# Query sketches in 64x64 tiles instead of 64x32, with the remainder's two batches as the outer loop

## The chip, the cores and the metric

The kernel runs on one core of a Trainium2 chip. The metric is device time in microseconds (us); lower is better. The engines are TensorE (PE, matrix products; its weight loads are listed as PEld), VectorE (DVE), ScalarE (ACT), GpSimd (POOL) and SyncE (SP, which issues most DMAs). All data are float32.

## The reference

Polysketch attention over 4 batches, 4 heads, 1088 tokens and 32 channels, then a GELU layer of 128 to 2048 to 128 channels over all 4352 tokens.

```
phi(x):  a = S1 x,  b = S2 x                # 8 numbers each
         features = outer(a, b)             # 64 numbers
kv  = phi(k)^T v          z = sum over tokens of phi(k)
x   = phi(q) kv / (phi(q) z + 1e-6)         # heads side by side: 128 channels
out = gelu(x w_in) w_out                    # 2048 hidden channels
```

What the change touches is the *query sketch*: for every query token and head, the products a and b with the two sketch matrices, and with them a product for the denominator.

## The kernel before, in words

**Chunks.** The queries go in chunks of 512 tokens of one batch: chunks 0 to 7 (two for each of the 4 batches). The last 64 tokens of all four batches together make chunk 8, the *remainder* (its halves have 128 columns where those of a main chunk have 256). Chunks 0 and 1 go another way at the start of the kernel; the sketch in question is made for chunks 2 to 8.

**The long middle.** From about 20 us on, the kernel is a list of steps, one for each chunk and each of 16 blocks of 128 hidden channels (`steps`, L962). In each step PE makes a hidden product (`hidden`, L715, product at L721), ScalarE takes it through GELU (L728), and PE multiplies earlier results by w_out (`two_products`, L792, product at L805, which uses a scheme with fewer products over sums that GpSimd makes at L770 to L773). What else has to be done for the chunks that follow (turning queries, sketches, key features, attention) is put into *slots* between the steps by hand (L964 to L1129). At the end of the kernel every engine is told to keep the order of the text (L1216 to L1222). So the order of PE's work is that of the program.

**The sketch** (`query_sketch`, L566, product at L578). `qT[n]` (from `query_turn`, L520) holds the chunk's queries with the channels of the heads in the partitions: rows 0 to 63 and 64 to 127 belong to two head pairs (`c`), the columns to two halves (`s`). `S_abc[b]` (L472; filled in `spread_sketches`, L475, and per batch in `sketch_of_z`, L489) is the stationary operand, 128 partitions x 2 (`fh`) x 2 (`r`) x 16: for each half `fh` of the first factor a and each head `r` of the pair, 4 numbers for a, 4 for the denominator and 8 for b. So 32 columns for each `fh`. Before the change a matmul takes 64 rows and 32 columns of weights, and 256 columns of queries. Its place in the array is the row half `c` and one of four column groups, `q4 = 2*s + fh`; that is a tile of 64x32, of which eight fit. A main chunk has 2 x 2 x 2 = 8 matmuls. In the remainder `m` is 2: each half `s` holds two batches `i` of 64 columns, whose weights differ, which makes 16 matmuls, with `s` as the outermost loop. The head pair `c` chooses the bank of PSUM, the column group its partitions.

**What reads it.** `query_outer` (L584) turns the sketch on VectorE (L590) and makes the query features. `attend` (L617; products at L633, in 64x32 tiles) multiplies them by kv; `take_x` (L638) copies the result with ScalarE (L644) to xT, which the hidden products of that chunk read.

**Where it stands.** At step t - 1 ahead of a chunk's own steps PE does, in this order:
- chunk 2 (L1082, L1083): the sums of kv (`kv_sum`, L440, product at L437 in 128x32 tiles), then the sketch.
- chunks 3 and 5 (`sketch_and_attend`, L1010): the sketch of n, the attention of n - 1, then the key features of the next batch (`features_of_all`, L970, product at L976 in 64x32 tiles).
- chunk 4 (`kv_and_attend`, L1048, then L1118): kv sums, attention of chunk 3, then the sketch.
- chunks 6 to 8 together (`last_sketches`, L1016): kv sums, attention of chunk 5, then the sketches of 8, 6 and 7.

The early part of the kernel has products in other tile shapes: `key_products` (L382) and `numerators_by_token` (L656) in 64x64 tiles, `expand_products` (L543) in 32x64. The products of hidden layers at L721 and L805 are in 128x64 tiles for most of the kernel.

Of the kernel before, what the change touches and what calls it, by code (L numbers as in the profile page):

```python
# [16 lines left out]
def kernel(  # L17
# [18 lines left out]
    pe, dve, act, pool, sp = nc.tensor, nc.vector, nc.scalar, nc.gpsimd, nc.sync  # L36
# [6 lines left out]
    NP = H // 2  # L43
# [23 lines left out]
    def work_banks():  # L67

        return wps.tile([128, 2, CW], FP, name="w_ps")
# [96 lines left out]
    def words(a):  # L166

        return (a, 1) if a.dtype == FP else (a.bitcast(U32), 2)
# [18 lines left out]
    for i, s in enumerate((S1, S2)):  # L187
        s, e = words(s)
# [283 lines left out]
    S_abc = [big.tile([128, 2, 2, 2 * R], FP, name=f"S_abc{b}") for b in range(B)]  # L472
# [44 lines left out]
    qT, qp, xT = {}, {}, {}  # L517
# [43 lines left out]
    def batch_of(n, s, i):  # L561
        return n // NCH if n < NMAIN else i * 2 + s
# [3 lines left out]
    def query_sketch(n, ps=None, tok=None):  # L566

        ps = work_banks() if ps is None else ps
        W = width[n]
        tok = ps[:, :, CW // 2:] if tok is None else tok  # L570
        m = 1 if n < NMAIN else B // 2
        N = W // 2 // m
        for s in range(2):
            for i in range(m):
                for fh in range(2):
                    for c in range(NP):
                        rows, q4 = slice(c * 64, (c + 1) * 64), 2 * s + fh
                        pe.matmul(ps[q4 * 32:(q4 + 1) * 32, c, i * N:(i + 1) * N],  # L578
                                  lhsT=S_abc[batch_of(n, s, i)][rows, fh].rearrange("p r x -> p (r x)"),
                                  rhs=qT[n].rearrange("p h j t -> p (h j t)")[rows, (s * m + i) * N:(s * m + i + 1) * N],  # L580
                                  start=True, stop=True)
        sketched[n] = ps, tok

    def query_outer(n):  # L584
# [308 lines left out]
    r = Rounding(SR)  # L893
# [116 lines left out]
    def sketch_and_attend(n):  # L1010

        ps = work_banks()
        query_sketch(n, ps)
        attend(n - 1, ps[:, :, CW // 2:])

    def last_sketches(b):  # L1016

        z_sum(b)
        fold_z(b)
        banks = work_banks()  # L1020
        kv = banks[:, 1, CW // 2 + 128:]
        kv_sum(b, kv)
        attend_products(NMAIN - 3, banks)
        query_sketch(NMAIN, banks[:, :, CW // 2:], banks)
        take_x(NMAIN - 3)
        take_kv(b, kv)
        two = work_banks()
        query_sketch(NMAIN - 2, two, banks)
        query_sketch(NMAIN - 1, two[:, :, CW // 2:], two)
        query_outer(NMAIN)  # L1030
# [59 lines left out]
    for n in range(3, NCHUNK):  # L1090

        t = (n - 1) * NF
# [69 lines left out]
    for t in range(len(steps) + LAG):  # L1162
# [35 lines left out]
        if t < len(steps):  # L1198
            n, fi = steps[t]
            hidden(n, fi, by_halves=t >= 18 and (n < NMAIN or fi < 5))  # L1200
        if t < len(steps) and steps[t][0] < NMAIN and steps[t][1] % NB == NB - 1:
            n, b = steps[t][0], steps[t][1] // NB
# [50 lines left out]
```

## Time and profile before

| | us |
|---|---|
| median of 3 runs | 259.8 (259.49 to 260.06) |
| the profiled execution's own time | 258.95 |
| its span, first to last instruction | 257.1 |
| PE busy | 253.1 (98%) |
| POOL, DVE, ACT busy | 164.1, 151.0, 115.2 |
| mean granted TensorE clock | 1.000 |

Busy times are unions: an engine with two instructions in flight is counted once. On PE many matmuls run side by side in different tiles of the array, and the record of each lasts from its start to the modelled arrival of its last result, so lengths of records overlap and don't add up to time. What adds up is the distance from the start of one group to the start of the next. The page's chain of work follows the end of the kernel back from what released each step. The timeline merges neighbouring instructions of one line and shape: start, length until the last end, and their number.

### The profile page before, as it was taken

How to read it: one execution, taken by the hardware profiler on the slowest of the kernel's cores; microseconds unless marked ns; L12 is line 12 of the kernel's file. 1: busy time of each engine (PE TensorE's matmuls, PEld its weight loads, DVE VectorE, ACT ScalarE, POOL GpSimd, SP SyncE). 2: the span in 40 equal slices, each digit the busy share in tenths (PEclk: the TensorE clock that was granted, in tenths of full speed). 3: DMA queues.
4: the chain of work that ended last, by engine and by line, in shares of the span. 5: the costliest groups of instructions: out<-in, count | busy, mean ns of one | idle time of the engine just before them, and what ended most of it. 6: DMA issues, size and time to landing. Idle time of an engine off the chain costs nothing.

```text
span 257.1 us, 5763 instructions
## 1 busy us (share of the span) xinstructions
PE 253.1 (98%) x2331; PEld 135.2 (53%) x2331; DVE 151.0 (59%) x313; ACT 115.2 (45%) x224; POOL 164.1 (64%) x173
## 2 busy tenths in 40 slices
PE   8999999999999999999999999999999999999995
PEld 7856444255454545454444455445544444445794
DVE  3896888969698996580278976399307000700330
ACT  4675766533535333533335332623444334433442
POOL 3504007799968777587758774787758777877300
PEclk9999999999999999999999999999999999999999
DMA  7479738720000101101000002000200200020020
GB/s 209 138 213 378 163 93 223 208 75 13 3 0 15 28 1 26 18 13 30 3 0 3 0 13 35 0 1 3 41 3 8 32 3 1 7 36 0 3 41 20
DMA packets 29594, 13.48 MB, mean 52 GB/s; under 512 B 21888, under 2 KB 27776, under 8 KB 29568
## 3 DMA queue, kind: packets, MB, share of 16 engines
q1 hardware_dynamic: 29392, 13.05, 20.4%
q8 instruction: 18, 0.29, 0.5%
q10 hardware_dynamic: 176, 0.07, 0.1%
q14 instruction: 8, 0.07, 0.1%
HBM read 10.88 MB, written 2.23 MB: 51 GB/s over the span
## 4 chain that ended last, share of the span: by engine, by line
PE 98%; ACT 0%; issue 0%
PE h_ps L721 45%; PE o_ps L805 33%; PE o_ps L856 5%; PE w_ps L853 3%; PE w_ps L437 1%; PE w_ps L578 1%; PE w_ps L888 1%; PE w_ps L633 1%; PE w_ps L543 1%; PE o_ps L426 1%; PE h_ps L735 1%; PE w_ps L976 1%; PE w_ps L656 0%; PE h_ps L333 0%; PE w_ps L333 0%; PE w_ps L467 0%
## 5 line engine op out<-in xcount | busy, mean ns | idle before, releaser
L721 PE MATMUL h_ps<-xT,w_in 128*64 128x512 f32 (+3 forms) x514 | 136.9, 576 | 0.0
L728 ACT ACTIVATE block<-h_ps 128x512 f32<-128x512 f32 (+1 forms) x128 | 73.0, 571 | 117.3 <-PE h_ps L721 115.3
L721 PEld LDWEIGHTS h_ps<-xT,w_in 128*64 128x64 f32 (+1 forms) x514 | 41.9, 142 | 30.6 <-issue 11.8
L805 PE MATMUL o_ps<-block,w_out 128*64 128x256 f32 x224 | 57.5, 379 | 0.0
L770 POOL TENSOR_TENSOR bits_low<-block 128x512 f32<-128x512 f32 x28 | 35.9, 1283 | 27.8 <-ACT block L728 27.8
L805 PEld LDWEIGHTS o_ps<-block,w_out 128*64 128x64 f32 x224 | 30.5, 137 | 38.0 <-issue 27.5
L771 POOL TENSOR_TENSOR bits_a<-block 128x512 f32<-128x512 f32 x28 | 35.8, 1278 | 12.0 <-ACT block L728 11.9
L820 DVE COPY sums<-o_ps 64x256 f32<-64x256 f32 x8 | 3.3, 416 | 60.7 <-PE o_ps L805 60.7
L772 POOL TENSOR_TENSOR bits_e<-bits_a,block 128x512 f32<-128x512 f32 x28 | 36.0, 1286 | 2.2
L773 POOL TENSOR_TENSOR bits_m<-block,bits_e 128x512 f32<-128x512 f32 x28 | 35.8, 1278 | 2.2
L805 PE MATMUL o_ps<-bits_a,small 128*64 128x256 f32 x112 | 28.8, 379 | 0.0
L805 PE MATMUL o_ps<-bits_low,small 128*64 128x256 f32 x112 | 28.8, 379 | 0.0
L805 PE MATMUL o_ps<-block,small 128*64 128x256 f32 x112 | 28.8, 379 | 0.0
L805 PE MATMUL o_ps<-bits_m,w_out 128*64 128x256 f32 x112 | 28.7, 379 | 0.0
L805 PEld LDWEIGHTS o_ps<-block,small 128*64 128x64 f32 x112 | 15.2, 137 | 17.9 <-issue 10.8
L805 PE MATMUL o_ps<-bits_e,small 128*64 128x256 f32 x112 | 17.0, 383 | 0.0
L856 PE MATMUL o_ps<-g,w_out 128*128 128x512 f32 (+1 forms) x34 | 16.5, 572 | 0.0
L805 PEld LDWEIGHTS o_ps<-bits_m,w_out 128*64 128x64 f32 x112 | 15.3, 137 | 0.0
L805 PEld LDWEIGHTS o_ps<-bits_a,small 128*64 128x64 f32 x112 | 15.2, 137 | 0.0
L805 PEld LDWEIGHTS o_ps<-bits_low,small 128*64 128x64 f32 x112 | 15.2, 137 | 0.0
L590 DVE STREAM_TRANSPOSE w_ps<-w_ps 128x512 f32<-128x512 f32 (+1 forms) x7 | 4.8, 687 | 17.1 <-ACT xT L644 12.7
L805 PEld LDWEIGHTS o_ps<-bits_e,small 128*64 128x64 f32 x112 | 7.7, 137 | 10.6 <-issue 8.8
(195 smaller groups left out, 303.7 us busy)
## 6 DMA issues: line engine op xcount, KB each, us to landing
block<-in_moe_w_in_dram SPq DMA_DIRECT2D x3, 512.0 KB, 8.3
block<-in_moe_w_out_dram SPq DMA_DIRECT2D x3, 512.0 KB, 12.3
k<-in_k_dram SPq DMA_DIRECT2D x12, 128.0 KB, 3.0
v<-in_v_dram SPq DMA_DIRECT2D x12, 128.0 KB, 3.3
q<-in_q_dram SPq DMA_DIRECT2D x24, 64.0 KB, 1.9
out_dram<-oT SPq DMA_DIRECT2D x21, 64.0 KB, 2.2
k<-in_k_dram SPq DMA_DIRECT2D x2, 256.0 KB, 3.2
q<-in_q_dram SPq DMA_DIRECT2D x2, 256.0 KB, 3.7
```

Of the source, the lines that this page charges most:

```text
L426: pe.matmul(ps[c * F:(c + 1) * F, r * 2 * D:r * 2 * D + C], lhsT=flat(k_p[0, r][:, t, c * 4 + ch * 2 + one]), rhs=v_aug[r][:, c, i, :C], s ...
L590: dve.transpose(out=tok, in_=ps[:, :, :H2])
L721: pe.matmul(ps[rows, :W], lhsT=w[:, rows], rhs=xT[n][:, :W], start=True, stop=True)
L728: act.activation(out=g_of[n, fi][:, :W], in_=ps[:, :W], func=ACT.Gelu)
L770: pool.tensor_sub(out=s[3], in0=a11, in1=a21)
L771: pool.tensor_add(out=s[1], in0=a21, in1=a22)
L772: pool.tensor_sub(out=s[2], in0=s[1], in1=a11)
L773: pool.tensor_sub(out=s[4], in0=a12, in1=s[2])
L805: pe.matmul(acc[n][bank][half * 64:(half + 1) * 64, col:col + HW], lhsT=fixed, rhs=moving, start=opens and e == 0 and name in "4715", stop ...
L820: dve.tensor_copy(out=N[lo, 0, one], in_=a0[lo, one])
L853: pe.matmul(o_of[n][i][:, :128], lhsT=g[:, i * 128:(i + 1) * 128], rhs=w_tile(w_out_sb, fi), start=first, stop=final)
L856: pe.matmul(o_of[n][:, cols], lhsT=w_tile(w_out_sb, fi), rhs=g[:, cols], start=first, stop=final)
```

## The change

In `query_sketch` the loop over `fh` goes: one matmul takes all 64 columns of the weights (both halves of the first factor) for a row half `c`, and writes 64 partitions, `s * 64` to `s * 64 + 64`. The results land in the same places as before. A main chunk has 4 matmuls instead of 8, the remainder 8 instead of 16. The loop over the remainder's batches `i` moves outside the loop over the halves `s`. Nothing else changes.

```diff
@@ query_sketch
         m = 1 if n < NMAIN else B // 2
         N = W // 2 // m
-        for s in range(2):
-            for i in range(m):
-                for fh in range(2):
-                    for c in range(NP):
-                        rows, q4 = slice(c * 64, (c + 1) * 64), 2 * s + fh
-                        pe.matmul(ps[q4 * 32:(q4 + 1) * 32, c, i * N:(i + 1) * N],
-                                  lhsT=S_abc[batch_of(n, s, i)][rows, fh].rearrange("p r x -> p (r x)"),
-                                  rhs=qT[n].rearrange("p h j t -> p (h j t)")[rows, (s * m + i) * N:(s * m + i + 1) * N],
-                                  start=True, stop=True)
+        for i in range(m):
+            for s in range(2):
+                for c in range(NP):
+                    rows = slice(c * 64, (c + 1) * 64)
+                    pe.matmul(ps[s * 64:(s + 1) * 64, c, i * N:(i + 1) * N],
+                              lhsT=S_abc[batch_of(n, s, i)][rows].rearrange("p f r x -> p (f r x)"),
+                              rhs=qT[n].rearrange("p h j t -> p (h j t)")[rows, (s * m + i) * N:(s * m + i + 1) * N],
+                              start=True, stop=True)
         sketched[n] = ps, tok
```

## The prediction

> **What bounds the kernel.** I read the views in this order: the page's chain of work, the matmul groups with shapes kept apart, the timeline of TensorE (PE) around each sketch, then the waits. The chain is PE alone, and the page gives PE an idle time of 0.8 us before its first matmul and hardly any after it:
>
> ```profile
> PE 98%; ACT 0%; issue 0%
> PEclk9999999999999999999999999999999999999999
> ```
>
> So a nanosecond that the sketch takes from PE's row, or adds to it, moves the end by as much. The granted clock stays at full speed. The groups give the size of the stage:
>
> ```profile
> L578 PE MATMUL w_ps<-qT,S_abc 64*32 64x256 f32 x96 | 3.8, 383 | 0.0
> L578 PE MATMUL w_ps<-qT_rem,S_abc 64*32 64x64 f32 x32 | 0.6, 219 | 0.0
> ```
>
> Each matmul of the text is two records (two passes of a float32 product): 6 chunks of 8 matmuls give x96, the remainder's 16 give x32. The whole stage is 4.4 us of 257.1. The means (383, 219 ns) are latencies and overlap; what counts is the distance from one group's start to the next one's. The timeline (start, length) shows it at the three kinds of place:
>
> ```profile
> 67.63 0.66 PE L578 MATMUL w_ps<-qT,S_abc 64*32 64x256 f32 x16
> 68.08 0.64 PE L633 MATMUL w_ps<-q_pT,kz 64*32 64x256 f32 x16
> 68.51 0.64 PE L976 MATMUL w_ps<-kT,S_ab 64*32 64x256 f32 x16
> 69.08 0.43 PE L805 MATMUL o_ps<-block,small 128*64 128x256 f32 x1
> ...
> 98.15 0.66 PE L633 MATMUL w_ps<-q_pT,kz 64*32 64x256 f32 x16
> 98.61 0.64 PE L578 MATMUL w_ps<-qT,S_abc 64*32 64x256 f32 x16
> 99.18 0.44 PE L805 MATMUL o_ps<-bits_e,small 128*64 128x256 f32 x2
> ```
> ```profile
> 154.05 0.66 PE L633 MATMUL w_ps<-q_pT,kz 64*32 64x256 f32 x16
> 154.50 0.52 PE L578 MATMUL w_ps<-qT_rem,S_abc 64*32 64x64 f32 x25
> ...
> 154.94 1.07 PE L578 MATMUL w_ps<-qT,S_abc 64*32 64x256 f32 x27
> 155.94 0.44 PE L805 MATMUL o_ps<-bits_e,small 128*64 128x256 f32 x2
> ```
> ```profile
> 11.43 0.67 PE L656 MATMUL h_ps<-kz,q_pT 64*64 64x33 f32 x32
> 11.92 0.65 PE L656 MATMUL o_ps<-kz,q_pT 64*64 64x33 f32 x32
> 12.50 1.12 PE L543 MATMUL w_ps<-qT,Srep 32*64 32x256 f32 x32
> 13.55 0.33 PE L694 MATMUL h_ps<-ident,x_tok 128*128 128x128 f32 x1
> ```
>
> The reader is to see that L578, L633 and L976, all in 64x32 tiles, follow each other without a break. A group of 16 passes there takes 0.43 us if one of the same tiles follows (68.08 to 68.51), but 0.57 if another tile shape follows (68.51 to 69.08).
>
> **The prices, from these rows.** The rest comes from the single records that the timeline merges.
> - A *wave*, one pass on every tile at once, is 215 ns for 256 columns whatever the number of tiles (two waves are the 0.43); 56 ns for 64 columns.
> - A *seam*, a change of tile shape, costs 91 to 94 ns over the wave: the last pass of 256 columns starts 306 ns before the next shape (306 - 215 = 91), of 512 columns 522 to 523 (429 for the wave: 94), of 64 columns 149 (93). It holds wherever the shape changes: 128x64 to 128x32, 128x64 to 64x32, 64x64 to 32x64. I take 91.
> - At a seam the *stagger* shows too: tiles start 6.7 ns apart, so the last of 8 lies 46 ns behind, the last of 4 20 ns. 215 + 215 + 46 + 91 + 0 = 567, the 0.57.
> - The *first weights* after a seam have nothing to hide behind: 25 ns for 32 columns (0.455 for L633 after L437, against 0.43), 51 for 64 (L543: four waves 860 + 51 + 46 + 91 = 1048; the row has 12.50 to 13.55 = 1.05).
>
> **The change part by part.** It removes half of the sketch's matmuls and weight loads (16 passes to 8 in a chunk, 32 to 16 in the remainder), each now 64 wide.
>
> *The main chunk's own time doesn't fall.* Eight tiles of 32 columns in two waves become four tiles of 64 columns in two waves, each pass still of 256 columns. Between two seams the old is 430 + 25 + 46 + 91 = 592, the new 430 + 51 + 20 + 91 = 592. Fewer instructions save 26 ns of stagger, and wider weights give them back.
>
> *Four seams are added.* Attend (L633) and the keys' features (L976) stay at 64x32, so where the sketch stood beside them it now has a seam of its own.
> - Chunk 3: sketch, attend, features were 1456 ns (67.627 to 69.083). Now: sketch 592; attend, first after a seam, 455; features, last before one, 568. Sum 1615: **+159**.
> - Chunk 5, the same order at 125.36: **+159**.
> - Chunk 4: attend, sketch were 1024 (98.152 to 99.176). Now each stands between seams, 592 + 592 = 1184: **+160**.
> - Chunks 8 (the remainder), 6 and 7, behind attend(5): 1894 now (154.046 to 155.940). The attend becomes 592. The remainder took 441 (154.502 to 154.943): with s as the outer loop, only 4 of the 8 tiles have work at a time. With i outside, all four 64x64 tiles have work in each wave: two batches by two passes make four waves of 56 = 225, and L656's waves of 58 on such tiles say that weights of 64 columns keep up. Chunks 6 and 7 keep four waves, 860. First weights 51, stagger 20, seam 91: 1247, and with the attend 1839: **-55**. The remainder gains 216, the seam gives most of it back.
> - Chunk 2 (55.90) has a seam on either side already. Its first weights load waits for a semaphore and the first pass starts 30 ns behind it; with 64 columns I take 57: **+27**, between 0 and 51.
>
> Sum: 159 + 159 + 160 - 55 + 27 = **+450 ns**. The profiled execution took 258.95 us around its span of 257.1, so 259.40; the median of the runs is 259.8, which the same 0.45 takes to **260.25**.
>
> *Cover.* Attend(2) and attend(4) end some 0.14 us later, but all that PE does between them and the first hidden product of the new x stays: ScalarE's copy (L644, 587 ns) has the same time as now. Behind attend(3) and attend(5) the copy gains time. VectorE's query_outer begins up to 0.14 later or 0.2 earlier and has many steps until its features are used. No DMA, wait or buffer is moved, and the writes to S_abc stay. If some cover were thin, the 0.14 would show as PE waiting for xT at a following L721.
>
> *The unknown prices.* No row has 64x32 beside 64x64, so this seam is bounded: below by none at all, above by the dearest in the trace, 195 - 56 = 139 ns (L437 to L578 at 55.9, which also waits for a semaphore). I take 91, since all the others lie at 91 to 94, also where the columns alone change (128x64 to 128x32). With no seam the parts become +25, +25, -26 and -241 (chunk 2 aside): -0.22, with chunk 2 -0.19. With 139 it is 0.45 + 4 x 0.048 = +0.64.
>
> The Trainium skill, TensorEngine Tiling (Array Packing), Key Properties, says that changing the tiling mode, and not just the tile, drains the engine. It gives no price, but speaks against this change: by it the unseen pair pays like the rest, the +0.45, and without it the sum would be the -0.19 above.
>
> The skill also has TensorE: Matmul & The Clock Gate, section "Wait — 56ns, not 53.3ns?": starts never come closer than about 25 ns. By that the remainder would go from 32 x 25 = 800 to 400 and the sum to +0.27. The records show 6.7 ns between tiles (154.502, 154.508), so here the rule does not hold, and 441 to 225 stands.
>
> **The rivals.**
> 1. *The drain is not paid between 64x32 and 64x64*, since both split the rows alike. For it: no row excludes it. Against it: 128x64 to 128x32 also share the rows and pay 94. Then -0.19: **259.6**.
> 2. *Dear seams: slower.* The four new seams (attend(2), sketch(4), attend(4), sketch(8)) cost 139 and not 91, since the next weights can't be fetched while the old shape runs. Price +0.64: **260.45**. It decides from a seam of 109 ns, where the sum passes +0.52. For it: the seam at 55.9. Against it: none of the four waits there for another engine.
> 3. *The two tiles of one row half run one after the other.* 64x64 with 256 columns is in no row, and L656's waves of 58 would have room for two streams of 33 columns. Then each main sketch takes four waves: 6 x 430 = +2.58, the remainder +0.22, in all **263.1**. Against it: L543 runs 32x64 tiles two to a row group at 215 a wave.
> 4. *The delay is taken in by slack, the change does nothing that can be seen*: **259.8**. For it: the matmuls' ends are modelled, so small stalls could hide in a busy PE. Against it: PE's waits have no fixed partner; ScalarE and GpSimd follow PE and shift with it.
>
> **How the numbers follow.** About 0.2% (0.52 us) is what a measurement of this kernel can tell from no change. Forecast 0.60; the sum lies just under that line, so 0.39 of it is "same" and 0.21 slower. Rival 1: 0.12 (same 0.08, faster 0.04). Rival 2: 0.15, slower. Rival 3: 0.04, slower. Rival 4: 0.09 (same 0.07, faster 0.02). Together faster 0.06, same 0.54, slower 0.40. The range goes from rival 1 less 0.1 (the spread of the runs, 259.49 to 260.06, is 0.3 to either side) to rival 2 plus the same: 259.5 to 260.9; rival 3 and the tails are left out.
>
> **What would show it.** L578 in rows 64*64 x48 and x16. Right: sketch to attend at chunk 3 goes from 0.45 to 0.59, attend to sketch at chunk 4 from 0.46 to 0.59, the remainder's start to that of chunks 6 and 7 from 0.44 to some 0.28 (the first weights with it), and PE's row from chunk 3's sketch to the end is longer by 0.4. Wrong: 0.48 and 0.43 at the first two places (rival 1), 0.64 (rival 2), a sketch of 0.9 or more (rival 3), or a later L721 that starts as early as now (rival 4). A wait of L721 for xT that wasn't there would be a cost that I have not counted.

## The result and the profile after

Over 14 runs of each, the changed kernel's median is 260.0 us (259.37 to 260.28), that of the kernel before 259.52 (258.73 to 260.37). The ratio is 1.0022 with a 95% interval of 1.0014 to 1.0031: slower by 0.57 us, between 0.36 and 0.80. The forecast was +0.45. It was put at 260.25 us because it started from 259.8, the median of three runs of the kernel before; over 14 runs that start is 259.52.

The profiled execution took 260.25 us around a span of 258.5, which is 1.33 more than before. Two thirds of that are not the change's. The second group of L543, ahead of any changed instruction, begins at 12.50 us before and at 13.38 after: 0.88 of scatter in the first part of the kernel (12.23 to 13.38 over all the profiles of this case). From that group to the start of the last matmul it is 241.192 us before and 241.628 after: **+436 ns**.

The timeline of PE in the changed kernel (start, length, engine, line) at chunk 3, at chunk 4 and at the remainder with chunks 6 and 7; lines behind the sketch have moved up by one:

```profile
68.51 0.66 PE L577 MATMUL w_ps<-qT,S_abc 64*64 64x256 f32 x8
69.10 0.66 PE L632 MATMUL w_ps<-q_pT,kz 64*32 64x256 f32 x16
69.56 0.64 PE L975 MATMUL w_ps<-kT,S_ab 64*32 64x256 f32 x16
70.12 0.43 PE L804 MATMUL o_ps<-block,small 128*64 128x256 f32 x1
```
```profile
99.19 0.66 PE L632 MATMUL w_ps<-q_pT,kz 64*32 64x256 f32 x16
99.78 0.66 PE L577 MATMUL w_ps<-qT,S_abc 64*64 64x256 f32 x8
100.38 0.44 PE L804 MATMUL o_ps<-bits_e,small 128*64 128x256 f32 x2
```
```profile
155.41 0.66 PE L632 MATMUL w_ps<-q_pT,kz 64*32 64x256 f32 x16
156.00 0.46 PE L577 MATMUL w_ps<-qT_rem,S_abc 64*64 64x64 f32 x16
156.28 1.05 PE L577 MATMUL w_ps<-qT,S_abc 64*64 64x256 f32 x16
157.26 0.44 PE L804 MATMUL o_ps<-bits_e,small 128*64 128x256 f32 x2
```

Sketch to attend at chunk 3 was 0.45 and is 0.59. Attend to sketch at chunk 4 was 0.46 and is 0.59. Only the remainder became shorter: from its start to the block of chunks 6 and 7 it was 0.44 and is 0.28 (the 0.44 holds five passes of chunk 6 already, of which more below; from the remainder's start to L804 it was 1438 ns and is 1258). In the single records, to the nanosecond, from the first pass of a place to the next L804:

| place | before | after | difference | forecast |
|---|---|---|---|---|
| chunk 2 | 597 | 592 | -5 | +27 |
| chunk 3: sketch, attend, features | 1456 | 1617 | +161 | +159 |
| chunk 4: attend, sketch | 1024 | 1185 | +161 | +160 |
| chunk 5, like 3 | 1456 | 1617 | +161 | +159 |
| attend(5), remainder, 6, 7 | 1894 | 1850 | -44 | -55 |
| sum | | | **+434** | **+450** |

The sum of the places is the +436 to within 2 ns. Nothing came later: no new wait shows on PE, and the busy times of the other engines are within 0.2 us of before.

### The profile page after: what moved, and what is told of

Its sections match the earlier page's. It is cut to its first block, busy times and chain, and to the rows that moved or that the text cites. A ratio compares the mean times of both kernels' runs of the same rounds, so it can differ in the third digit from the quotient of the medians.

```text
span 258.5 us, 5635 instructions
## 1 busy us (share of the span) xinstructions
PE 254.4 (98%) x2267; PEld 135.0 (52%) x2267; DVE 151.1 (58%) x313; ACT 115.4 (45%) x224; POOL 164.3 (64%) x173
## 4 chain that ended last, share of the span: by engine, by line
PE 98%; ACT 0%; issue 0%
PE h_ps L720 45%; PE o_ps L804 33%; PE o_ps L855 5%; PE w_ps L852 3%; PE w_ps L632 1%; PE w_ps L437 1%; PE w_ps L577 1%; PE w_ps L887 1%; PE w_ps L543 1%; PE o_ps L426 1%; PE h_ps L734 1%; PE w_ps L975 1%; PE w_ps L655 0%; PE h_ps L333 0%; PE w_ps L333 0%; PE h_ps L655 0%
## 5 line engine op out<-in xcount | busy, mean ns | idle before, releaser
L804 PE MATMUL o_ps<-block,w_out 128*64 128x256 f32 x224 | 57.5, 379 | 0.0
L804 PEld LDWEIGHTS o_ps<-block,w_out 128*64 128x64 f32 x224 | 30.5, 137 | 38.0 <-issue 27.5
L804 PE MATMUL o_ps<-bits_low,small 128*64 128x256 f32 x112 | 28.8, 379 | 0.0
L804 PE MATMUL o_ps<-block,small 128*64 128x256 f32 x112 | 28.8, 379 | 0.0
L804 PE MATMUL o_ps<-bits_a,small 128*64 128x256 f32 x112 | 28.8, 379 | 0.0
L804 PE MATMUL o_ps<-bits_m,w_out 128*64 128x256 f32 x112 | 28.7, 379 | 0.0
L804 PEld LDWEIGHTS o_ps<-block,small 128*64 128x64 f32 x112 | 15.2, 137 | 17.9 <-issue 10.8
L804 PE MATMUL o_ps<-bits_e,small 128*64 128x256 f32 x112 | 17.0, 383 | 0.0
L804 PEld LDWEIGHTS o_ps<-bits_m,w_out 128*64 128x64 f32 x112 | 15.3, 137 | 0.0
L804 PEld LDWEIGHTS o_ps<-bits_a,small 128*64 128x64 f32 x112 | 15.2, 137 | 0.0
L804 PEld LDWEIGHTS o_ps<-bits_low,small 128*64 128x64 f32 x112 | 15.2, 137 | 0.0
L804 PEld LDWEIGHTS o_ps<-bits_e,small 128*64 128x64 f32 x112 | 7.7, 137 | 10.6 <-issue 8.8
```

The lines of the kernel that those rows point to most:

```text
L804: pe.matmul(acc[n][bank][half * 64:(half + 1) * 64, col:col + HW], lhsT=fixed, rhs=moving, start=opens and e == 0 and name in "4715", stop ...
```

## The experiments

The theory is the prediction's: the sketch's own waves cost the same in both shapes, and a seam (a change of tile shape) costs about 0.14 us at each place where one is added, with the first weights and the stagger. The rivals: wide tiles cost by themselves; the order of work costs and not the shape; and, on the remainder, two readings of why it became shorter. A ratio is a run's time over that of the kernel before, with its 95% interval. For each run the local figure is the distance between first passes in PE's records. The last matmul's start is counted from the second L543 as above.

**1. The remainder's loop order alone**, narrow tiles.

```diff
-        for s in range(2):
-            for i in range(m):
+        for i in range(m):
+            for s in range(2):
                 for fh in range(2):
```

> The kernel before with the remainder's batches i as the outer loop and nothing else: still 64x32 tiles, still 32 passes, but all eight tiles have work from the start. If the remainder's old 441 ns came from only four of the eight tiles having work at a time (the prediction's reading), it falls to four waves of 56, 225 ns, and the kernel gets 0.2 us faster. If they came from the number of passes (32 at 13.8 ns each, whatever the tiles), it stays at 430 to 450 ns and the time does not change. The seams stay those of before: 1456 ns at chunk 3, 1024 at chunk 4.

Ratio 1.0000 (0.9989 to 1.0011); to the last matmul 241.157, 35 ns less than before. The timeline around the remainder in this kernel:

```profile
154.85 0.53 PE L578 MATMUL w_ps<-qT_rem,S_abc 64*32 64x64 f32 x28
155.16 0.40 PE L578 MATMUL w_ps<-qT,S_abc 64*32 64x256 f32 x1
155.18 0.22 PE L578 MATMUL w_ps<-qT_rem,S_abc 64*32 64x64 f32 x1
...
155.23 1.10 PE L578 MATMUL w_ps<-qT,S_abc 64*32 64x256 f32 x28
156.26 0.44 PE L805 MATMUL o_ps<-bits_e,small 128*64 128x256 f32 x2
```

From the remainder's start to L805 it is 1403 ns, where before has 1438. The first 16 passes go as the prediction thought, two waves of eight in 112 ns; the rest take until 373. So the old 441 did not come from idle tiles alone.

**2. Wide tiles with the old loop order.**

```diff
-        for i in range(m):
-            for s in range(2):
+        for s in range(2):
+            for i in range(m):
                 for c in range(NP):
```

> The changed kernel with the halves s outside the batches i again: 64x64 tiles, 16 passes in the remainder, but only two of the four tiles have work at a time. If the number of tiles with work decides, the remainder takes eight waves of 56, 450 ns, and the kernel is 0.2 us slower than the changed one (0.65 slower than before). If the number of passes decides, 16 at 14 to 17 ns, 225 to 270 ns, and the time is that of the changed kernel (0.43 slower than before). The main chunks are as in the changed kernel.

Ratio 1.0019 (1.0007 to 1.0030). The remainder, with its two tiles at a time in program order:

```profile
155.75 0.47 PE L577 MATMUL w_ps<-qT_rem,S_abc 64*64 64x64 f32 x16
156.04 1.06 PE L577 MATMUL w_ps<-qT,S_abc 64*64 64x256 f32 x16
157.03 0.44 PE L804 MATMUL o_ps<-bits_e,small 128*64 128x256 f32 x2
```

The remainder's start to chunk 6 is 282 ns, the same as in the changed kernel; the place is 13 ns longer. Its records come in waves of four (0, 7, 27, 34, then 107, 114, 134, 140 ns), though in program order only two tiles have work before the second half `s` is reached. The profile doesn't name a pass's tile, but such a pass holds its tile for 56 to 58 ns (that far apart come the waves of run 1 and of the changed kernel), so four starts within 34 ns need four tiles: PE starts passes of the second half while the first half's later passes still wait. So the loop order is worth next to nothing with wide tiles, and the prediction's reason for the remainder (idle tiles) is refuted. What is left is the halved number of passes (with wider weights).

**3. One more seam at chunks 3 and 5**, the changed kernel with attend ahead of the sketch.

```diff
 def sketch_and_attend(n):
         ps = work_banks()
-        query_sketch(n, ps)
         attend(n - 1, ps[:, :, CW // 2:])
+        query_sketch(n, ps)
```

> The changed kernel with the order attend, sketch, key features at chunks 3 and 5 (it was sketch, attend, key features): the same instructions, but the 64x64 sketch now stands between two groups of 64x32 tiles, so each of these places has one more seam. Seams as the cause: 592 + 592 + 592 = 1776 ns at each place where the changed kernel has 1617, +0.16 twice, so 0.32 slower than the changed kernel and 0.75 slower than before. If wider passes or fewer instructions were the cause and not the order, nothing changes against the changed kernel (0.43 slower than before).

Ratio 1.0093 (1.0076 to 1.0109), far more than either theory gave. The timeline of PE at chunk 3, with the idle time and its releaser at the end of the line:

```profile
68.46 0.66 PE L632 MATMUL w_ps<-q_pT,kz 64*32 64x256 f32 x16
69.87 0.66 PE L577 MATMUL w_ps<-qT,S_abc 64*64 64x256 f32 x8 [0.74 <-ACT xT L643]
70.46 0.66 PE L975 MATMUL w_ps<-kT,S_ab 64*32 64x256 f32 x16
71.05 0.43 PE L804 MATMUL o_ps<-block,small 128*64 128x256 f32 x1
```

The sketch waits for ScalarE's copy of xT, which reads the other half of the same banks and now stands ahead of it in the text: attend to sketch is 1408 ns instead of 592, twice 0.82 us. The run mixed two causes and was made again without the wait:

**4. The same order, the copy behind the sketch** (the edit is shown against run 3).

```diff
-        attend(n - 1, ps[:, :, CW // 2:])
+        attend_products(n - 1, ps[:, :, CW // 2:])
         query_sketch(n, ps)
+        take_x(n - 1)
```

> As the run before with the sketch in the middle (attend, sketch, key features at chunks 3 and 5, 64x64 tiles), but ScalarE's copy of the attention's result comes behind the sketch in the text, so the sketch no longer waits for it (that wait was 0.8 us at each of the two places). Seams as the cause: no wait, attend 592 + sketch 592 + features 592 = 1776 ns at both places, 0.32 slower than the changed kernel, 0.75 slower than before. If the order costs nothing, 1617 ns as in the changed kernel, 0.43 slower than before.

Ratio 1.0027 (1.0015 to 1.0038). At chunk 3:

```profile
67.35 0.66 PE L632 MATMUL w_ps<-q_pT,kz 64*32 64x256 f32 x16
67.94 0.66 PE L577 MATMUL w_ps<-qT,S_abc 64*64 64x256 f32 x8
68.54 0.66 PE L975 MATMUL w_ps<-kT,S_ab 64*32 64x256 f32 x16
69.13 0.43 PE L804 MATMUL o_ps<-block,small 128*64 128x256 f32 x1
```

Three groups of 0.59: 1777 ns at each of the two places. To the last matmul 241.948, **+756 ns** against the expected 0.75. The instructions are those of the changed kernel; only the number of seams is different.

**5. The same order with narrow tiles**, in the kernel before.

> The same order (attend, sketch, key features, copy behind the sketch) in the kernel before, with 64x32 tiles all through: no seam is added, so 1456 ns at chunks 3 and 5 and the time of before. If the order itself costs, about 0.3 slower than before.

Ratio 0.9993 (0.9984 to 1.0003); to the last matmul 241.193, 1 ns from before:

```profile
67.95 0.66 PE L633 MATMUL w_ps<-q_pT,kz 64*32 64x256 f32 x16
68.41 0.64 PE L578 MATMUL w_ps<-qT,S_abc 64*32 64x256 f32 x16
68.84 0.64 PE L976 MATMUL w_ps<-kT,S_ab 64*32 64x256 f32 x16
69.41 0.43 PE L805 MATMUL o_ps<-block,small 128*64 128x256 f32 x1
```

With one shape the order is free. Runs 4 and 5 together leave the seam, and neither the order nor the sketch, as the cause.

**6. Wide tiles only where they add no seam, or one that the remainder pays for.**

```diff
+        if n in (2, NMAIN - 2, NMAIN - 1, NMAIN):
             ... the loops of the changed kernel
+        else:
             ... the loops of the kernel before
```

> 64x64 tiles only for the chunks 2, 6, 7 and the remainder, 64x32 tiles as before for chunks 3, 4 and 5. Seams as the cause: the three places with +160 ns are back to 1456, 1024 and 1456 ns, and what is left is -5 at chunk 2 and -44 at chunks 8, 6 and 7: 0.05 faster than before, no difference that can be measured. If 64x64 tiles cost by themselves, more than half of the 0.43 stays.

Ratio 0.9992 (0.9982 to 1.0002). Chunks 3, 4 and 5 are back to 1456, 1024 and 1456 within 1 ns; the last place is 1850. To the last matmul 241.144, 48 ns less than before. It is the shortest of all by PE's row, and the timing cannot tell it from the kernel before.

**7. Wide tiles for the remainder alone** (`if n == NMAIN` in the edit of run 6).

> 64x64 tiles for the remainder alone, 64x32 for all main chunks as before. Chunks 3 and 4 are back to 1456 and 1024 ns. At the last place there are two new seams, ahead of the remainder and behind it: attend 592, remainder 282 + 20 + 91, chunks 6 and 7 25 + 860 + 46 + 91 = 1022, in all 2007 where before has 1894: 0.11 slower than before at this place. Were 64x64 tiles dear by themselves and seams free, the place would be shorter than before by the remainder's gain, 0.16 to 0.2.

Ratio 1.0004 (0.9992 to 1.0015); to the last matmul 241.307, **+115 ns**:

```profile
154.17 0.66 PE L643 MATMUL w_ps<-q_pT,kz 64*32 64x256 f32 x16
154.76 0.46 PE L578 MATMUL w_ps<-qT_rem,S_abc 64*64 64x64 f32 x16
155.16 1.09 PE L588 MATMUL w_ps<-qT,S_abc 64*32 64x256 f32 x32
156.18 0.44 PE L815 MATMUL o_ps<-bits_e,small 128*64 128x256 f32 x2
```

The place is 593 + 391 + 1025 = 2009 ns (2007 expected). From its start to the block of chunks 6 and 7 the remainder is shorter here than before (391 to 441, with a seam in the 391), and the place is longer: the two seams eat more than the wide tiles give.

**8. The changed kernel again.**

> The changed kernel once more, for its span: the stretch from PE's products at L543 on is 0.43 longer than before, and the 0.88 that its first profile had more in the first 13 us is scatter of the loads and does not come back in this size. Time 0.4 to 0.5 slower than before. If the 0.88 belongs to the change, the span is again 1.3 longer.

Ratio 1.0015 (1.0004 to 1.0026), span 257.7. The second L543 begins at 12.68, and from there to the last matmul it is 241.630: +438 ns, the first profile's figure within 2 ns. The 0.88 did not come back.

**9. More passes, the same columns**, in the kernel before: each matmul of the remainder cut in two.

```diff
                     for c in range(NP):
+                        for x in range(m):
-                        pe.matmul(ps[..., c, i * N:(i + 1) * N], ...
+                            pe.matmul(ps[..., c, i * N + x * (N // m):i * N + (x + 1) * (N // m)], ...
```

> The kernel before, in 64x32 tiles and its old order, with each matmul of the remainder cut into two of 32 columns: 64 passes instead of 32, the same columns in all. If the remainder is held by the spacing of passes (16.6 ns each behind the first 16 or so), 32 more passes cost 530 ns: from its start to the next L805 it is 1970 ns where before has 1438, and the kernel is 0.5 slower. If it is held by columns per tile, which stay the same, 1438 and no change.

Ratio 1.0083 (1.0060 to 1.0106), 2.1 us, which is neither; from the remainder's start to L806 it is 3640 ns:

```profile
154.89 0.90 PE L579 MATMUL w_ps<-qT_rem,S_abc 64*32 64x32 f32 x63
...
155.64 1.11 PE L579 MATMUL w_ps<-qT,S_abc 64*32 64x256 f32 x28
157.98 0.62 PE L579 MATMUL w_ps<-qT,S_abc 64*32 64x256 f32 x3 [1.23 <-issue]
158.53 0.44 PE L806 MATMUL o_ps<-bits_e,small 128*64 128x256 f32 x2
```

In the middle of chunks 6 and 7 no pass starts for 1604 ns (156.38 to 157.98), and the profile shows nothing that PE waits for. The queue of instruction loads had a 16 KB load under way from 155.00 to 156.41. Such a load alone makes no gap: the kernel before has one at the same place, from 154.32 to 155.84, and PE goes on.

**10. The same with spare products ahead**, which shift the program against these loads. The spare products compute nothing that is used.

```diff
+    def spare_products():
+        for ps in (work_bank(), work_bank()):
+            for i in range(16):
+                ... pe.matmul(ps[:32, :32], lhsT=zeros, rhs=zeros, start=True, stop=True)
+    at(72, spare_products)
```

> The run before this one (the remainder in 64 passes) had a gap of 1.6 us in PE's row at 156.4, in the middle of chunks 6 and 7, with a 16 KB load of instructions in flight. Here 32 spare products of zeros (64 passes, 128 instructions with their weight loads, 8 KB of instructions, in a bank that nobody reads) stand 8 steps earlier, which shifts the loads by half of one against the program. If the gap comes from a load that falls into a dense stretch of short products, it goes (or moves), and the place takes some 1.75 us from the remainder's start to the next L805; the spare products cost about 2 us where they stand. If the gap belongs to the 64 passes themselves, it stays and the place takes 3.6 us.

```profile
157.73 0.80 PE L579 MATMUL w_ps<-qT_rem,S_abc 64*32 64x32 f32 x59
...
158.44 1.08 PE L579 MATMUL w_ps<-qT,S_abc 64*32 64x256 f32 x27
159.44 0.44 PE L806 MATMUL o_ps<-bits_e,small 128*64 128x256 f32 x2
```

The gap is gone (the nearest loads run from 152.84 to 153.80 and from 159.06 on), and from the remainder's start to L806 it is 1710 ns, 272 more than before for 32 passes more: 8.5 ns a pass. (A single execution, 262.42 us beside 259.77 before; the spare products cost 2.5 us where they stand.) So the remainder depends on the number of passes at unchanged columns, though at half the 16.6 ns that run 9 expected.

## Why the prediction was right, and where its reason was not

**That PE's row is the end** held: +434 at the five places, +436 from the second L543 to the last matmul, and a ratio whose interval, 0.36 to 0.80 us, holds the forecast. (The upper end of the range, 260.9, doesn't follow from its own words: 260.45 and 0.1 are 260.55, with 0.3 they are 260.75. The measured 260.0 lies inside all of these.)

**That the main chunk's own time doesn't fall** held: alone between two seams the wide sketch takes 592 ns, as forecast, and the narrow one 597. Half the instructions bought 5 ns.

**The four seams** held in number and price. The last pass of 256 columns starts 305 to 306 ns before the next shape, also between 64x32 and 64x64, so 90 to 91 over the wave. Each of the three places is 161 where 159 and 160 stood. Rival 1 (no drain between the two) fell with the first of these figures. Rival 2 (dear seams) fell too: not one of the four is above 306. Rival 3 (tiles of one row half one after the other) would have made the sketch 1 us long; it is 0.59. Rival 4 (slack) fell in the last matmul's start. The rule that the prediction took from the Trainium skill, TensorEngine Tiling (Array Packing), Key Properties, that a change of tiling mode drains the engine, agrees with these 90 to 91 ns for the pair that the old trace did not show.

**Chunk 2** was the first mis-sized term: +27 forecast, -5 measured. The first pass was expected to start later behind wider weights, but it starts 30 ns behind its weight load with 32 columns and 31 with 64, and the last pass of L437 to the first of the sketch is 195 ns in both kernels. What is left is the sketch's own 597 to 592.

**The remainder's gain** was right in size and wrong in its reason. Forecast were 276 ns to the start of chunk 6, and 282 came. The step that failed is "with s as the outer loop, only 4 of the 8 tiles have work at a time". Run 1 gave all eight tiles work and gained 35 ns instead of 216. Run 2 took the loop order back and lost 13. The order of the loops is worth little, since PE starts passes on free tiles ahead of earlier passes that wait for theirs: the profile of run 1 shows a pass of chunk 6 (155.16) ahead of passes of the remainder (155.18 and later), and in the program the whole remainder stands ahead of chunk 6.

The trace of the kernel before showed this already, in lines between those that the prediction shows:

```profile
154.81 0.40 PE L578 MATMUL w_ps<-qT,S_abc 64*32 64x256 f32 x1
154.82 0.22 PE L578 MATMUL w_ps<-qT_rem,S_abc 64*32 64x64 f32 x2
...
154.89 0.25 PE L578 MATMUL w_ps<-qT_rem,S_abc 64*32 64x64 f32 x3
```

Chunk 6 starts there 312 ns behind the remainder's first pass, not 441, and the first five passes of the remainder start within 46 ns, within the 56 for which a pass of 64 columns holds its tile; so a fifth tile had work by then. The sum came out all the same, because it took the old time of the whole place as measured and had the four new waves right (58 ns each, where 56 were taken). The idle tiles were only its explanation of the old time.

On the order of starts the Trainium skill is at odds with the runs: TensorE: Matmul & The Clock Gate, section The mechanism (in Part 3), has matmuls start strictly in program order; here the measurement decides. What was gained comes with 16 passes instead of 32. Runs 9 and 10 show from the other side that more passes for the same columns cost time. What sets the 8.5 to 17 ns between passes there (weight loads, the supply of instructions, a tile's turn) was not separated and stays open.

## What to carry to other kernels

In the main chunks, fewer and wider matmuls in waves of the same number and length were worth 5 ns: count waves, not instructions. Before a tile shape is changed, look at what stands beside it: here every added change of shape cost 0.14 to 0.16 us with its first weights and stagger, more than the halved instruction count saved in a main chunk. The only gain of size was where passes are short (64 columns) and their number matters; it is best taken at a place that already has a seam on either side.

## What the runs showed of the hardware that was not expected

- PE starts passes out of program order between tiles: 34 ns after its first pass, run 2's remainder was on all four tiles (read from the starts), while its program has eight passes for two tiles first.
- A dense stretch of short passes was interrupted, perhaps by the loading of PE's own instructions: run 9 has a gap of 1604 ns, all four of its times (261.23 to 261.69 us) fit it, and it is gone in run 10 with the program shifted by 128 instructions. The Trainium skill, Runtime: NRT & Kernel Launch, section Instruction fetch mechanics, has these loads in blocks of 16 KB and hidden behind the issue of instructions; if a load is the cause, here one was not. This is the likeliest reading and not proved: PE went on 1.57 us after the load's end, which nothing in the profile explains, and run 10 is one execution.
- A matmul waits for a reader of other columns in the same two banks if the reader stands ahead of it in the text (run 3, 0.82 us twice); with the reader behind it the wait is gone (run 4). The wait is on a semaphore of the program; whether the chip needs it no run shows.
